# A fixed table of the order in place of a greedy plan: attention, a feed-forward layer and a soft mixture of experts on one Trainium2 core

## The chip, the core and the metric

The kernel runs on one core of one Trainium2 chip. The metric is the device time of one execution in microseconds (us), the median of several runs. A core has five engines, each with its own queue of instructions that are worked off in order: TensorE (PE in the rows; its weight loads are PEld), VectorE (DVE), ScalarE (ACT), GpSimd (POOL) and SyncE (SP), which in this kernel issues every DMA. An engine that waits for a semaphore holds up all that is queued behind the waiting instruction.

## What is computed

Three stages, one after the other; the last two have weights that are shared by all tokens.

```python
# attention: q, k, v are (4, 8, 576, 64)
q_rot, k_rot = (rotate(q), rotate(k))
scores = scale * np.matmul(q_rot, k_rot.transpose(0, 1, 3, 2))
scores = scores - np.max(scores, axis=-1, keepdims=True)
attn = np.exp(scores)
attn = attn / (np.sum(attn, axis=-1, keepdims=True) + 1e-09)
x = np.matmul(attn, v)                 # then (2304, 512)
# feed-forward: w_in (512, 2048), w_out (2048, 512)
h = x @ w_in
x = (np.maximum(h, 0.0) + alpha * np.minimum(h, 0.0)) @ w_out
# soft mixture: phi (512, 32), 8 experts, 4 slots each, w1 (8, 512, 1024), w2 (8, 1024, 512)
logits = x @ phi
d = softmax(logits, 0); slot_input = d.T @ x
slot_out[e] = np.maximum(slot_input[e] @ w1[e], 0.0) @ w2[e]
return softmax(logits, 1) @ slot_out
```

## The kernel before

**Tiling.** Attention goes over 4 batches `b` and 4 pairs `p` of heads; a pair has five row blocks `s` of 128 rows (the fifth, `s == 4`, holds the last 64 rows of both heads). For each row block and head there are: the scores on TensorE (`plain`, L419, for batch 0, in float32; `scores`, L432, for the later batches, of split values) into a PSUM tile `st`, of which there are two; the row maximum on VectorE (`top`, L437); the exponential on ScalarE (`expo`, L442); sum and reciprocal on VectorE (L449, L450); the division on GpSimd (`norm`, L474). The result then has to be transposed: in batch 0 on TensorE (`turn`, L495), for the later batches by 32x32 blocks on VectorE (`block`, L482) and through device memory, with a `save` (L519, `sc<-tb`) for each row block and a `fetch` (L528, `ET<-sc`, four DMAs) for each two. `pv` (L574) multiplies with v. Before that, q and k are rotated (`prep_qk`, L322 and L330): pair 0 of batch 0 on VectorE, all others on GpSimd.

**Weights.** `prep_w` brings `w_in` and `w_out` from raw 64-bit data into tiles (L643, L645, L647 on VectorE), scales and splits them (`bnd`, `hi`, `diag` on ScalarE, `rest` L268 and L269 on TensorE), in sixteen steps that lie within batch 0 of the attention, since the first feed-forward chunk needs both.

**Feed-forward and dispatch.** The tokens are eight blocks of 256 (two a batch) and a ninth of all the last rows. Each has sixteen chunks `f` (`mm1`, L735: twelve matmuls), whose results are activated (L743 on ScalarE, L748 on VectorE), transposed, and added up in the running softmax over tokens (`dispatch_events`).

**Tail.** When the attention's buffers are free (`att_done`), SP loads `w_out` again (`wor`, L1103, 16 transfers) and all the experts' weights (`xw`, L1158) into one pool of tiles; VectorE converts `w_out` (`late_w`), TensorE forms the slots' input (`px`, L1209), the experts (`ph` L1262, `po` L1316) and the result (`pf`, L1427), and SP stores.

**What sets the order.** The kernel first makes a list of 2900 operations. Each has an engine, an estimated cost, a due time, the operations that it depends on, and the buffers (slots of a class, such as two of `st` or three of `pm`) that it takes and uses. `Plan.order` then plays the list through: at each moment an idle engine takes, of the operations that are ready and whose slots are free, the one with the earliest due time. The order in which operations were started is the order in which their instructions are written, and so the order in each engine's queue. Semaphores are set by the data: what an instruction waits for follows from the tiles that it reads and writes. At the end:

```python
    for o in plan.order():
        o.fn()
```

## Time and profile before

| | |
|---|---|
| time before, median of 3 runs (lowest to highest) | 657.65 us (656.19 to 658.19) |
| span of the profiled execution | 663.7 us |
| TensorE busy | 609.5 us (92%) |
| VectorE busy | 462.9 us (70%) |
| ScalarE busy | 373.6 us (56%) |
| GpSimd busy | 269.9 us (41%) |
| mean DMA rate | 221 GB/s, 146.6 MB |
| first matmul | at 11.64 us |
| last matmul ends | at 657.3 us |

The profiled execution is 6.1 us longer than the median of the unprofiled runs. The page gives each engine's busy time, 40 slices of the span, and the chain of work that ended last: 71% of that chain is TensorE, 9% VectorE, 8% DMA, 5% GpSimd. A matmul that runs slowly counts as busy, so a busy TensorE is not TensorE at its peak. The trace tells each instruction's start, its length and what ended the idle time ahead of it.

### The profile page before, as it was taken

To read this page: it belongs to the slowest core of one execution; us is meant where nothing else is said; L and a number is where in the kernel's file an instruction comes from. 1 tells how busy PE (TensorE), PEld (TensorE's weight loads), DVE (VectorE), ACT (ScalarE), POOL (GpSimd) and SP (SyncE) were. 2 spreads that over 40 slices of the span, in tenths; PEclk is the share of its full clock that TensorE was granted. 3 is DMA by queue.
4 is the path that set the end of the run, shared out by engine and by line. 5 is a ranking of instruction groups with operands and counts; after the bars stand their busy time and mean duration, and the time that the engine had idled before them with its cause. 6 is when DMAs were issued, how large, how long until landed. Compare 5 with 4: busy or idle time off the path is not lost.

```text
span 663.7 us, 13899 instructions
## 1 busy us (share of the span) xinstructions
PE 609.5 (92%) x5232; PEld 429.7 (65%) x5232; DVE 462.9 (70%) x1000; ACT 373.6 (56%) x900; POOL 269.9 (41%) x262
## 2 busy tenths in 40 slices
PE   1899988999999999898899989989999999997994
PEld 1554543656878687586777867778677787773352
DVE  5859496788777867886677777867663788853442
ACT  2666775676686766766758576766554232331121
POOL 0669584467446547575574644522320000001000
PEclk9778895999999999999999999999999999997996
DMA  9954263633298887878888786667643993669998
GB/s 337 339 182 147 69 221 122 199 118 108 82 250 203 252 221 213 236 231 264 226 229 206 216 235 169 190 174 176 170 128 96 375 409 137 255 254 369 403 337 287
DMA packets 70371, 146.60 MB, mean 221 GB/s; under 512 B 5921, under 2 KB 35233, under 8 KB 70305
## 3 DMA queue, kind: packets, MB, share of 16 engines
q1 hardware_dynamic: 70304, 145.72, 70.2%
q8 instruction: 41, 0.67, 0.4%
q14 instruction: 26, 0.20, 0.1%
HBM read 108.73 MB, written 29.88 MB: 209 GB/s over the span
## 4 chain that ended last, share of the span: by engine, by line
PE 71%; DVE 9%; DMA 8%; POOL 5%; ACT 3%; issue 2%; SPq 2%; POOLq 0%; DVEq 0%; ACTq 0%
PE ph L735 25%; PE pv L574 12%; PE st L432 6%; PE st L419 5%; DMA ET<-sc 3%; PE pt L754 3%; DMA xw<-in_moe_w_dram 3%; PE lg L772 3%; PE pt L495 3%; POOL xn L322 2%; PE po L1316 2%; PE pu L891 2%; PE pc L538 2%; POOL e L474 2%; DVE mm L437 2%
## 5 line engine op out<-in xcount | busy, mean ns | idle before, releaser
L474 POOL TENSOR_SCALAR e<-e,mm 128x576 f32<-128x576 f32 x144 | 121.1, 851 | 163.6 <-DVE mm L450 100.6
L735 PEld LDWEIGHTS <-w 128*128 128x128 f16 x1728 | 163.7, 98 | 33.3 <-issue 12.4
L735 PE MATMUL ph<-xt,w 128*128 128x256 f16 x1536 | 183.8, 273 | 0.5 <-DVE g L748 0.3
L437 DVE TENSOR_REDUCE mm<-st 128x1 f32<-128x576 f32 x144 | 106.4, 744 | 32.1 <-PE st L432 15.5
L442 ACT ACTIVATE e<-st,mm 128x576 f32<-128x576 f32 x144 | 106.3, 738 | 26.9 <-DVE mm L437 22.6
L743 ACT ACTIVATE rl<-ph 128x256 f32<-128x256 f32 x144 | 55.0, 382 | 91.6 <-PE ph L735 88.1
L322 POOL TENSOR_TENSOR xn<-xn,tabs 128x576 f32<-128x576 f32 x60 | 92.1, 1551 | 34.1 <-DMA xn<-in_k_dram 16.2
L748 DVE SCALAR_TENSOR_TENSOR g<-rl,oma,ph 128x256 f32<-128x256 f32 x144 | 68.0, 472 | 40.4 <-ACT rl L743 39.1
L574 PE MATMUL pv<-ET,vt 128*64 128x256 f32 x512 | 62.3, 385 | 12.2 <-DMA ET<-sc 5.7
L432 PE MATMUL st<-ks,qs 128*128 128x288 f32 x384 | 72.5, 314 | 0.5 <-ACT e L442 0.5
L482 DVE STREAM_TRANSPOSE tb<-e 128x512 f32<-128x512 f32 x96 | 66.8, 700 | 5.6 <-POOL e L474 4.1
L419 PE MATMUL st<-ks 64*128 64x288 f32 (+1 forms) x168 | 51.0, 498 | 14.0 <-DVE ks L330 11.6
L432 PEld LDWEIGHTS st<-ks,qs 128*128 128x128 f32 x384 | 55.2, 192 | 4.5 <-issue 2.0
L574 PEld LDWEIGHTS pv<-ET,vt 128*64 128x64 f32 x512 | 35.3, 136 | 33.1 <-ACT qs L340 4.2
L419 PEld LDWEIGHTS st<-ks 64*128 64x128 f32 (+1 forms) x168 | 27.9, 210 | 28.6 <-DVE ks L330 11.6
L584 ACT ACTIVATE xt<-pv,vb 128x256 f16<-128x256 f32 x32 | 15.1, 473 | 43.8 <-PE pv L574 43.8
L759 ACT ACTIVATE gt<-pt 128x512 f32<-128x512 f32 x56 | 33.1, 596 | 11.5 <-PE pt L754 10.9
L325 POOL TENSOR_TENSOR xn<-xn 128x576 f32<-128x576 f32 x24 | 36.2, 1508 | 1.0
L449 DVE TENSOR_SCALAR mm<-mm 128x2 f32<-128x2 f32 (+1 forms) x80 | 28.5, 357 | 11.2 <-ACT e L442 10.8
L495 PE MATMUL pt<-idf,e 128*128 128x128 f32 x192 | 33.3, 307 | 3.2 <-POOL e L474 2.9
L495 PEld LDWEIGHTS pt<-idf,e 128*128 128x128 f32 x192 | 24.9, 158 | 16.3 <-POOL e L474 8.9
L587 DVE SCALAR_TENSOR_TENSOR xt<-pv,vb,xt 128x256 f16<-128x256 f32 x32 | 15.4, 481 | 28.1 <-ACT xt L584 27.9
(181 smaller groups left out, 896.6 us busy)
## 6 DMA issues: line engine op xcount, KB each, us to landing
sc<-tb SPq DMA_DIRECT2D x48, 512.0 KB, 4.6
ET<-sc SPq DMA_DIRECT2D x96, 256.0 KB, 5.7
xw<-in_moe_w_dram SPq DMA_DIRECT2D x42, 512.0 KB, 9.9
xn<-in_k_dram SPq DMA_DIRECT2D x16, 576.0 KB, 5.7
xn<-in_q_dram SPq DMA_DIRECT2D x16, 576.0 KB, 4.1
wraw<-in_moe_w_in_dram SPq DMA_DIRECT2D x8, 1024.0 KB, 9.8
wraw<-in_w_out_t_dram SPq DMA_DIRECT2D x8, 1024.0 KB, 5.2
wor<-in_moe_w_out_dram SPq DMA_DIRECT2D x16, 512.0 KB, 10.4
```

Of the source, the lines that this page charges most:

```text
L322: eng.tensor_tensor(e["x"][:, w], e["x"][:, w], tabs[:, (0 if z == "q" else 2) + w], ALU.mult)
L419: nc.tensor.matmul(st[to, j, at:at + w], x, k[rows, z:z + w], start=True, stop=True)
L432: nc.tensor.matmul(st[:, j, 0:288], r["q"][:, 768 * h + 128 * s:768 * h + 128 * s + 128].bitcast(F32R), r["k"][:, a, h, ks].bitcast(F32R), ...
L437: nc.vector.tensor_reduce(c["mm"][:, h:h + 1], c["st", h][:, :, 0:288], axis=AX.XY, op=ALU.max, negate=True)
L442: nc.scalar.activation(c["e"][:, h].rearrange("p (a n) -> p a n", a=2), c["st", h][:, :, 0:288], AF.Exp, bias=c["mm"][:, h:h + 1], accum_o ...
L474: nc.gpsimd.tensor_scalar(c["e"][:, h], c["e"][:, h], c["mm"][:, 6 + h:7 + h], 1.0, ALU.mult, ALU.mult)
L482: nc.vector.transpose(out=c["tb"][:, :, h].rearrange("p (q m) j -> p q m j", q=4), in_=c["e"][:, h, 64 * h:64 * h + 512].rearrange("p (m q ...
L495: nc.tensor.transpose(c["pt", h][:, i], c["e"][:, h, 64 * h + 128 * i:64 * h + 128 * i + 128], idf)
L574: nc.tensor.matmul(pv[r], v[k, 4 * h + i if i < 4 else 8], x, start=(i == 0), stop=(i == 4))
L735: nc.tensor.matmul(ph, wi[j][:, wp, kc, 128 * fo:128 * fo + 128], xt[:, xp, kc, :], start=(n == 0), stop=(n == 3 * KC - 1),)
L743: nc.scalar.activation(c["r"], c["ph"], AF.Relu, scale=-1.0)
L748: nc.vector.scalar_tensor_tensor(blk["g", j][:, fo, :], c["r"], oma[:, f:f + 1], c["ph"], ALU.mult, ALU.add)
```

## The change

The class `Plan` no longer plays the list through. Its `order` unpacks a table, a string of some 6,000 characters, that gives for each place the number of the operation that stands there. The 2900 operations, their tiles and their functions stay the same, and each engine gets the same instructions as before; only their order differs. The lists of dependencies get the entries that the greedy play had kept by itself (an activation after the one that allocates its tile, transposes of a group after the first, turns on the two `h1` buffers); they are used to assert that the table respects them. The first lines of the table stand for all of it.

```diff
-import bisect
-import heapq
+import base64
+import zlib
+ORDER = (
+    "c-mc72S5}@7v48}1-RqrN*BdO5yW0l6jT%g5*3x-SQ0fP(HMJ)Eo!167+Wl{`-"
...
         for d in deps:
             d.after.append(o)
-        o.wait += len(deps)
+        o.deps, o.wait = o.deps + list(deps), o.wait + len(deps)
...
     def order(self):
-        ready = {o.eng: [] for o in self.ops}
-        free = {e: 0.0 for e in ready}
...
-        while events:
...
-                    o = next((o for o in ready[e] if self.fits(o)), None)
...
+        raw = zlib.decompress(base64.b85decode(ORDER))
+        n, at, order = len(raw) // 2, 0, []
+        for lo, hi in zip(raw[:n], raw[n:]):
+            at = (at + lo + 256 * hi) % 65536
+            order.append(self.ops[at])
+        done, room, left = set(), dict(self.room), {}
...
+        for o in order:
+            assert all(d in done for d in o.deps) and o not in done, "an operation stands before one that it needs"
...
-        o = op(DVE, 480, d, act, [o, oma_op], uses=[s_pm, s_r, s_g])
+        o = op(DVE, 480, d, act, [o, oma_op, blk["g_op"][4 * j] if fo else None], uses=[s_pm, s_r, s_g])
...
-            blk["gt_op"].append(op(ACT, 600, due + 100 if late else d, turned, [o], uses=[s_pt, s_gt]))
+            blk["gt_op"].append(op(ACT, 600, due + 100 if late else d, turned, [o, blk["gt_op"][f // 8 * 4] if f % 8 > 1 else None], uses=[s_pt, s_gt]))
...
+    turns = []
+
+    def in_turn(take, *users):
+
+        for old in turns[-1:]:
+            plan.also(take, [old[0]])
+        for old in turns[-2:-1]:
+            plan.also(take, old)
+        turns.append([take, *users])
...
-            x = op(PE, 430, D2 - 10, turn, [x], takes=[s_pm], uses=[s_pm, s_h])
+            x, h = op(PE, 430, D2 - 10, turn, [x], takes=[s_pm], uses=[s_pm, s_h]), x
+            in_turn(h, x)
```

Within the operations a line of the changed kernel stands 16 lines higher than before: L403 there is L419 here, L503 is L519, L512 is L528.

**Place 1, the start of the program.** SP's queue from its first DMA, before; `tabs` are the tables of the rotation (k's first, then q's), `xn` the raw k or q of a pair, `vt` v, `wraw` raw weights:

```order
L235 DMA tabs<-in_rope_dram 128x1152
L319 DMA xn<-in_k_dram 128x1152
L235 DMA tabs<-in_rope_dram 128x1152
L319 DMA xn<-in_q_dram 128x1152
L291 DMA vt<-in_v_dram 128x576 x2
L621 DMA wraw<-in_moe_w_in_dram 128x4x512
L291 DMA vt<-in_v_dram 128x576
```

and now (the first `tabs` are q's, the second k's):

```order
L219 DMA tabs<-in_rope_dram 128x1152
L303 DMA xn<-in_k_dram 128x1152
L303 DMA xn<-in_q_dram 128x1152
L275 DMA vt<-in_v_dram 128x576
L219 DMA tabs<-in_rope_dram 128x1152
L605 DMA wraw<-in_moe_w_in_dram 128x4x512
L275 DMA vt<-in_v_dram 128x576 x3
```

The second table now comes behind q and behind one load of v. On VectorE the rotation follows, before (k, then q, each two products and a sum) and now (four products, q's first, then k's sum and q's sum):

```order
L322 TENSOR_TENSOR xn<-xn,tabs 128x576 x2
L330 TENSOR_TENSOR ks<-xn 128x576
L322 TENSOR_TENSOR xn<-xn,tabs 128x576 x2
L330 TENSOR_TENSOR ks<-xn 128x576
L437 TENSOR_REDUCE mm<-st 128x1
```

```order
L306 TENSOR_TENSOR xn<-xn,tabs 128x576 x4
L314 TENSOR_TENSOR ks<-xn 128x576 x2
L627 TENSOR_SCALAR w_164<-wraw 128x8x128
L629 SCALAR_TENSOR_TENSOR w_164<-wraw,w_164 128x8x128
L421 TENSOR_REDUCE mm<-st 128x1
```

Two steps of the first weight conversion moved ahead of the first row maximum.

**Place 2, TensorE at the start of batch 0.** `st<-ks` are scores, `pt<-idf,e` the transposes of finished rows, `rest` the remainder of a weight tile, `top` a maximum over partitions. Before:

```order
L419 MATMUL st<-ks 128x288 x8
L229 MATMUL top<-idf,vb 128x128
L229 MATMUL top<-idf,mws 128x128
L495 MATMUL pt<-idf,e 128x128 x8
L538 MATMUL pc<-idf,e 128x128
L419 MATMUL st<-ks 128x288 x4
L268 MATMUL rest<-w_177,dg 128x512
```

Now:

```order
L403 MATMUL st<-ks 128x288 x8
L213 MATMUL top<-idf,mws 128x128
L403 MATMUL st<-ks 128x288 x4
L479 MATMUL pt<-idf,e 128x128 x4
L522 MATMUL pc<-idf,e 128x128
L252 MATMUL rest<-w_164,dg 128x512
L253 LDWEIGHTS neg
L253 MATMUL rest<-w_164,neg 128x512
L479 MATMUL pt<-idf,e 128x128 x4
```

The third row block's scores moved ahead of the transposes of the first, and the first weight remainder between these transposes.

**Place 3, SP in batch 2, pair 1.** `sc<-tb` is a save, `ET<-sc` a fetch of two saved row blocks (four DMAs), the first fetch here belongs to pair 0. Before:

```order
L528 DMA ET<-sc 32x8x256 x4
L519 DMA sc<-tb 128x1024
L319 DMA xn<-in_k_dram 128x1152
L519 DMA sc<-tb 128x1024
L291 DMA vt<-in_v_dram 128x576
L363 DMA ks<-xn 64x576 x4
L519 DMA sc<-tb 128x1024
L528 DMA ET<-sc 32x8x256 x4
L519 DMA sc<-tb 128x1024
```

Now:

```order
L512 DMA ET<-sc 32x8x256 x4
L503 DMA sc<-tb 128x1024
L275 DMA vt<-in_v_dram 128x576
L503 DMA sc<-tb 128x1024
L303 DMA xn<-in_k_dram 128x1152
L512 DMA ET<-sc 32x8x256 x4
L503 DMA sc<-tb 128x1024 x2
```

The fetch of pair 1 stood behind the third row block's save and a stack of four DMAs; now it follows the second save with one load between, and the third save is behind it.

## Rows read from the trace of the kernel before

**Rows 1.** The page: busy us of each engine, share of span, instructions.

```profile
PE 609.5 (92%) x5232; PEld 429.7 (65%) x5232; DVE 462.9 (70%) x1000; ACT 373.6 (56%) x900; POOL 269.9 (41%) x262
```

**Rows 2.** Busy time by stretch: PE, PEld, DVE, ACT, POOL; then clock, DMA share, GB/s.

```profile
0.00:157.10 157.10, 133.41 (x670) 75.78 (x670) 114.69 (x210) 99.20 (x223) 93.41 (x76) 0.86 0.55 187
157.10:514.00 356.90, 341.53 (x3078) 264.87 (x3076) 259.83 (x570) 236.46 (x585) 173.86 (x181) 1.00 0.72 197
```

**Rows 3.** The same view of three stretches in batch 0.

```profile
25.06:42.12 17.06, 15.20 (x41) 7.94 (x41) 10.75 (x20) 9.97 (x20) 13.59 (x11) 0.50 0.71 248
62.60:72.85 10.25, 10.25 (x42) 6.16 (x41) 7.70 (x16) 6.05 (x14) 9.40 (x8) 0.50 0.66 224
100.15:117.22 17.07, 15.29 (x36) 6.65 (x36) 9.88 (x16) 8.88 (x20) 8.25 (x6) 0.50 0.32 109
```

**Rows 4.** Chain that ended last: start us, us, what.

```profile
31.07 2.21 PE st L419 x4
...
117.66 1.16 PE st L419 x4
...
157.31 1.34 PE ph L735 x12
```

**Rows 5.** TensorE's waits, 11 to 157 us: us in total, times, longest.

```profile
PE rest L268 <- ACT dg L262: 4.0, 3, 2.5
PE pt L495 <- POOL e L474: 2.9, 5, 1.5
PE st L419 <- ACT e L442: 2.2, 2, 1.7
```

**Rows 6.** TensorE in order of time: start, us, what, [idle before].

```profile
26.71 2.08 PE L268 MATMUL rest<-w,dg 128*128 128x512 f32 x2 [2.52 <-ACT dg L262]
...
61.61 0.66 PE L495 MATMUL pt<-idf,e 128*128 128x128 f32 x4 [1.46 <-POOL e L474]
...
100.45 2.08 PE L268 MATMUL rest<-wx,dg 128*128 128x512 f32 x2 [1.37 <-ACT dg L262]
```

**Rows 7.** Groups of TensorE by shape: busy us, mean ns, idle ahead, releasers.

```profile
L574 PE MATMUL pv<-ET,vt 128*64 128x256 f32 x512 | 62.3, 385 | 12.2 <-DMA ET<-sc 5.7 <-DVE qs L347 2.8 <-ACT qs L340 1.7
```

**Rows 8.** TensorE in order of time, batch 2, pair 1.

```profile
300.38 0.77 PE L432 MATMUL st<-ks,qs 128*128 128x288 f32 x4
...
330.72 1.95 PE L574 MATMUL pv<-ET,vt 128*64 128x256 f32 x16 [2.79 <-DVE qs L347]
```

**Rows 9.** SP in order of time, the same place.

```profile
313.60 0.32 SPq L519 DMA_DIRECT2D sc<-tb  x1
...
320.94 2.33 SPq L528 DMA_DIRECT2D ET<-sc  x4
```

**Rows 10.** VectorE in order of time, the start.

```profile
6.37 1.43 DVE L322 TENSOR_TENSOR xn<-xn,tabs 128x576 f32<-128x576 f32 x2 [3.78 <-DMA xn<-in_k_dram]
...
9.37 1.43 DVE L322 TENSOR_TENSOR xn<-xn,tabs 128x576 f32<-128x576 f32 x2 [0.79 <-DMA xn<-in_q_dram]
...
10.83 0.76 DVE L330 TENSOR_TENSOR ks<-xn 128x576 f32<-128x576 f32 x1
```

**Rows 11.** TensorE's waits over the span, the row of later batches' scores.

```profile
PE st L432 <- ACT e L442: 0.5, 2, 0.4
```

**Rows 12.** Busy time by stretch, the tail.

```profile
540.00:560.00 20.00, 20.00 (x291) 16.07 (x288) 17.34 (x42) 6.25 (x19) 0.00 (x0) 1.00 0.68 269
...
620.00:640.00 20.00, 19.61 (x254) 9.80 (x250) 6.90 (x31) 4.27 (x9) 0.00 (x0) 1.00 1.01 391
```

**Rows 13.** VectorE and GpSimd in order of time, the start of batch 0.

```profile
15.91 1.22 DVE L645 SCALAR_TENSOR_TENSOR w<-wraw,w 128x1024 int32<-128x1024 int32 x1
...
22.13 4.18 POOL L322 TENSOR_TENSOR xn<-xn,tabs 128x576 f32<-128x576 f32 x2 [1.95 <-DMA xn<-in_k_dram]
...
22.74 2.31 DVE L645 SCALAR_TENSOR_TENSOR w<-wraw,w 128x1024 int32<-128x1024 int32 x1
...
43.86 1.41 POOL L322 TENSOR_TENSOR xn<-xn,tabs 128x576 f32<-128x576 f32 x1
```

More of the change, by code (lines that the diff above doesn't have):

```diff
@@ L73, in also @@
             d.after.append(o)
-        o.wait += len(deps)
-    @staticmethod
-    def lag(a, b):
-        if a.eng is None or b.eng is None:
-            return 0
-        if a.eng == b.eng == "DMA" and b.back:
-            return 3300
-        if a.eng == b.eng:
-            return {"DVE": 127, "POOL": 102}.get(a.eng, 0)
-        if b.eng == "DMA":
-            return 1420
-        if b.eng == "PE":
-            return {"DMA": 2400, "POOL": 240}.get(a.eng, 230)
-        return {"DMA": 2400, "PE": 230 if b.eng == "ACT" else 197, "POOL": 65}.get(a.eng, 160)
@@ L90, in pe_end @@
-    def pe_end(self, at, cost):
-        while cost > 1e-6:
-            edge = self.window + 3413.0
-            if at >= edge:
-                if self.busy >= 0.96 * 3413.0:
-                    self.warm = True
-                elif self.busy < 0.33 * 3413.0:
-                    self.warm = False
-                self.window, self.busy = edge, 0.0
-                continue
-            k = 1.0 if self.warm else 2.0
-            step = min(cost * k, edge - at)
-            at, cost, self.busy = at + step, cost - step / k, self.busy + step
-        return at
@@ L155, in fits @@
-    def fits(self, o):
-        need = {}
-        for s in o.takes:
-            need[s.cls] = need.get(s.cls, 0) + 1
-        return all(self.room[c] >= k for c, k in need.items())
+        o.deps, o.wait = o.deps + list(deps), o.wait + len(deps)
+    def order(self):
+        raw = zlib.decompress(base64.b85decode(ORDER))
[4 more added lines that the diff above has]
+        done, room, left = set(), dict(self.room), {}
+        for o in self.ops:
+            for s in set(o.uses):
+                left[s] = left.get(s, 0) + 1
+        for o in order:
+            assert all(d in done for d in o.deps) and o not in done, "an operation stands before one that it needs"
+            for s in o.takes:
+                room[s.cls] -= 1
+                assert room[s.cls] >= 0, "a buffer is taken before it is free"
+            for s in set(o.uses):
+                left[s] -= 1
+                room[s.cls] += not left[s]
+            done.add(o)
+        assert len(order) == len(self.ops)
+        return order
```

89 lines of the change are left out of this document (46 added, 43 removed).

## The prediction

> **What bounds the kernel now.** I read the page's busy times first: TensorE 92% of the span, no other engine over 70% [rows 1]. The table by stretch then says where the missing time lies. Up to 157.1 us, where the first feed-forward chunk starts, TensorE works 133.4 us at a mean clock of 0.86; from there to 514 us it works 341.5 of 356.9 us at full clock [rows 2]. So the first stretch is the loose one, and there two things are lost. One is the clock: in three stretches of 17.06, 10.25 and 17.07 us the granted clock is 0.50, the 1.2 GHz level, while TensorE is busy for 15.20, 10.25 and 15.29 us, 40.7 us together [rows 3]. The same scores take 2.21 us there and 1.16 us at 2.4 GHz [rows 4]; if all work there shrank so, 40.7 x (1 - 1.16 / 2.21) = 19.3 us is the whole price of the slow clock. The other is waiting: 4.0 us for the diagonal that the weight remainder needs, 2.9 us for rows that GpSimd divides, 2.2 us for the exponential [rows 5], about 11.5 us with the view's small rows. The clock fell at 25.06, 62.60 and 100.15 us [rows 3]; each time TensorE had just been idle or was so, for 2.52, 1.46 and 1.37 us [rows 6].
>
> In the long middle stretch nearly all waiting is one kind: 12.2 us ahead of `pv`, which needs the fetched rows [rows 7]. What the row names there as releaser (a VectorE line) had been done; it was the transfer: one such `pv` starts at 330.72 us after 2.79 us of idleness [rows 8], 9.8 us after its fetch began to be issued at 320.94 us [rows 9].
>
> The same instructions run before and after, so only waits and the clock can change. I count the order's pieces between two operations and price each at the median that it has in the trace at full clock, as 1.16 us for a score of batch 0 and 1.34 us for a feed-forward chunk [rows 4]. Such a sum is the cover that an operation has while its input is made elsewhere.
>
> **The start: +1.4 us.** Before, the first score waits for q's last sum, which ends at 10.83 + 0.76 = 11.59 us. Two tables and two inputs of equal size are loaded; the first two are there at 6.37 us and all four at 9.37 us [rows 10], so one takes 1.5 us. Now the table that k needs is fifth, behind a load of v of half that size: all is there at 9.37 + 0.75 = 10.12 us. Behind it stand two products and two sums, 1.43 + 2 x 0.76 = 2.95 us [rows 10], so the first score can start at 13.07 us instead of 11.6. I take +1.4 us (bounds 0 and +3, if the weight steps that VectorE now does ahead of the first maximum wait for their load).
>
> **Waits in batch 0: -6 us.** For the 36 transposes of batch 0 the cover between a row's score and its transpose is 10.6 us in the mean before and 14.5 us now, and it is larger in 34 of 36. The one that waited until 61.61 us [rows 6] had 14.4 us of cover and has 15.9 us now, 1.5 us more, which is its wait. So the TensorE side is done well. But VectorE works 114.7 us and GpSimd 93.4 us of these 157.1 us [rows 2], and if TensorE runs ahead, they become late. I take half of the 11.5 us (bounds -11.5 and 0).
>
> **The clock in batch 0: -8 us.** If the waits ahead of the three falls go, the falls may go with them; nothing says all will, and the middle stretch has longer waits, as the 2.79 us [rows 8], with the clock at 1.00 throughout [rows 2]. I take somewhat under half of 19.3 us (bounds -19.3, and +5 for another fall of 10 us at half clock). VectorE stays a floor: 114.7 us of work in a stretch that would then be 157.1 + 1.4 - 6 - 8 = 144.5 us is 79%, against 73% now, which is feasible.
>
> **The fetches: -10 us.** Two things changed for the 24 `pv` that wait for a fetch. First, SP: before, the fetch stood in 14 of 24 places behind a save of the next row block or a load whose release comes more than 1 us of TensorE work later than its own, now in 4; the third place of the order shows one. In the trace its save was issued at 313.60 us and the fetch 7.3 us later [rows 9]. Second, the cover from the last score to `pv` is 23.3 us in the mean before and 28.0 us now. For the `pv` at 330.72 us it is 25.1 and 30.3 us: its scores ended at 301.15 us, so it needed 29.6 us [rows 8]. Five of the 24 have less cover than before, the two of batch 2, pair 3 by 3.1 and 0.7 us, so I leave 2 of the 12.2 us [rows 7] (bounds -12.2 and -4).
>
> **Score buffers: +2 us.** With two `st` tiles a score waits until the exponential two scores earlier is done. In the middle stretch the cover for that is shorter than the time which the softmax took in the trace at 19 places, by 29 us in sum; before it was 6 places and 7 us, which cost 0.5 us [rows 11], since VectorE and ScalarE then serve that row earlier. 29 x 0.5 / 7 = 2 us (bounds 0 and +29).
>
> **The tail: +2 us.** The last attention `pv` now has 458 us of TensorE work ahead of it and its like, where it had 451, so the tail's loads start 7 us of work later. Between 540 and 560 us the DMA engines are busy for 0.68 of the time, so part of the delay is taken up by idle transfers; from 620 to 640 us they are full at 1.01 [rows 12], and there a delay shows. SP also has loads of the second expert matrix among those of the first. By the count both orders have issued the same number of loads when the last dispatch starts. I take +2 us (bounds -3 and +7).
>
> **Sum:** 1.4 - 6 - 8 - 10 + 2 + 2 = -18.6 us, on the profiled execution 663.7 - 18.6 = 645.1 us. That execution is 6.1 us longer than the median of 657.65 us, and I take the same step off the median: 639.0 us.
>
> **Rivals.** *VectorE and GpSimd take the first stretch back.* VectorE's shift of the raw weights takes 1.22 us alone and 2.31 us while GpSimd multiplies, whose two products take 4.18 us there, and one 1.41 us elsewhere [rows 13]. Packed closer, both overlap more; if the 14 us of waits and clock are eaten so, 1.4 - 10 + 2 + 2 = -4.6 us and 653.0 us. The Trainium skill (SBUF — State Buffer, section Who interferes with whom) has a rule that makes this likelier: the port pair that VectorE shares with GpSimd is locked for a whole instruction by whichever begins first. By that rule the loss grows with every overlap that a closer order makes; the rows above agree that such pairs exist, and no run here yet shows how many more there will be. For this rival speaks that VectorE is already the second most used engine; against it, that its share only has to rise from 73% to 79%. Chance 0.2.
>
> *The first stretch is cured.* All 11.5 us of waits and all 19.3 us of slow clock go, and all 12.2 us ahead of `pv`: 1.4 - 11.5 - 19.3 - 12.2 + 2 + 2 = -37.6 us, 620 us. VectorE would then be busy for 114.7 of 127.7 us, 90%; that hardly leaves room for its own waits. Chance 0.08.
>
> *The score buffers bind.* The place is the middle stretch: if VectorE and ScalarE don't serve the closer scores sooner, the 29 us are paid in full instead of 2: -18.6 + 27 = +8.4 us and 666 us. It turns the sign when more than 20.6 of the 29 us are paid. Against it is the row of 0.5 us. Chance 0.08 for slower by it, and 0.04 more for slower by late loads in the tail, which would need over 20 us there.
>
> *The order changes, the time doesn't.* Gains in the middle are given back where SP or the tail's full DMA engines set the pace anyway: 657.65 us. Chance 0.05.
>
> **Chances and range.** The forecast, between about 628 and 649 us, has 0.55. Faster by over 0.3% (about 2 us, what a measurement of this kernel can tell from no change): 0.55 + 0.2 + 0.08 and a little of what lies between, 0.83; within 0.3%: 0.05; slower: 0.12. For 8 in 10 the range holds the forecast, the first rival and the nearer part of the second: 625 to 655 us.
>
> **What would show it.** In the changed profile the first matmul should start near 13.0 us; the first feed-forward chunk (L735 moved up 16 lines, so L719) near 144 us instead of 157.1; one or two stretches at clock 0.50 within batch 0 instead of three; TensorE's idle time ahead of `pv` (L558) near 2 us instead of 12.2; its wait for the exponential in the later batches near 2 us. The distance from the last `pv` to the end, 150 us before, should stay within some 5 us. The prediction is wrong if the first chunk doesn't start earlier although the waits are gone (then VectorE or GpSimd sets the pace), if the clock falls as often as before, or if what batch 0 gains is lost while TensorE waits for the experts' weights.

## The result, and the profile after

The changed kernel takes 625.87 us (median of 4 runs, 620.67 to 630.32) beside 657.12 us for the kernel before: a ratio of 0.947 (95% interval 0.941 to 0.954). Two more measurements gave 0.948 (0.945 to 0.952) and 0.945 (0.942 to 0.949). The forecast of 639.0 us had the direction right; of the 31 to 37 us by which the three medians fell it had 18.6. On the 657.65 us that it started from, the three ratios give 621.6 to 623.7 us, below the 625 us at which its range ended. The kernel before is the less steady of the two: in four later calls its median was 661 to 662 us, with single runs from 654.62 to 668.47 us, and its profiled execution, with a span of 663.7 us, lies in that spread (a span in a trace is some 2 us shorter than the time of the same execution). Some runs below are compared across these four calls; the kernel before had 661.0 to 661.8 us in each of them. The changed kernel stays between 620.67 and 630.32 us.

The page's busy times after (as [rows 1]):

```profile
PE 582.6 (94%) x5232; PEld 421.9 (68%) x5232; DVE 458.4 (74%) x1000; ACT 370.8 (60%) x900; POOL 264.8 (43%) x262
```

TensorE has the same 5232 instructions and is busy for 26.9 us less: for the most part a slow clock had counted as work. The table by stretch (columns as in [rows 2]; the cuts are the first feed-forward chunk and the end of the last attention `pv`), of the first trace of the changed kernel:

```profile
0.00:135.00 135.00, 114.51 (x670) 67.47 (x671) 111.21 (x199) 96.64 (x219) 88.27 (x73) 0.99 0.60 209
135.00:481.50 346.50, 344.50 (x3140) 271.23 (x3140) 262.83 (x586) 238.74 (x593) 173.79 (x184) 1.00 0.75 206
481.50:618.90 137.40, 123.63 (x1424) 83.16 (x1424) 84.38 (x215) 35.39 (x89) 2.75 (x5) 0.97 0.90 341
```

and of a later one (the run `after_third` below):

```profile
0.00:137.40 137.40, 112.06 (x670) 65.88 (x671) 111.66 (x199) 96.91 (x219) 91.95 (x73) 1.00 0.60 206
137.40:485.00 347.60, 344.53 (x3140) 271.32 (x3138) 264.00 (x586) 239.03 (x593) 174.40 (x184) 1.00 0.76 206
485.00:622.80 137.80, 123.09 (x1428) 83.21 (x1424) 84.47 (x215) 35.46 (x89) 2.75 (x5) 0.98 0.90 340
```

Against [rows 2]: in the first stretch the same 670 matmuls are busy for 114.5 and 112.1 us instead of 133.4 us, at a clock of 0.99 and 1.00 instead of 0.86. In the middle TensorE idles 2.0 and 3.1 us instead of 15.4 us, although 62 more matmuls now lie in it: five feed-forward chunks of 1.34 us [rows 4] and two matmuls of 0.22 us, an estimated 7.1 us of work. The tail lasts 137.4 and 137.8 us where it was 149.7 us; 7.1 us of that is the work that moved.

The clock column of these tables leaves something out. A trace has no record of the clock before its first rise, and the column counts that time as 1.00. The first rise stands at 21.64 us in the first trace of before, and at 30.33, 27.22 and 27.95 us in the traces of `after`, `after_again` and `after_third`. Until then TensorE works at half speed, the 1.2 GHz level: in the first trace of before one score follows the other after 0.48 us ahead of the rise and after 0.24 us behind it, and in the first trace of the changed kernel the same two matmuls take, ahead of the rise and later:

```profile
26.16 1.92 PE L252 MATMUL rest<-w,dg 128*128 128x512 f32 x2
...
82.57 1.12 PE L252 MATMUL rest<-w,dg 128*128 128x512 f32 x2
```

With this start and the falls together, TensorE is busy at half speed for 8.3 + 40.7 = 49.0 us of batch 0 before, for 15.6 + 3.4 = 19.0 us in the first trace of the changed kernel (which has one fall, of 3.41 us at 64.47 us) and for 12.8 us in the later one. If half of each is the price of the slow clock, it fell from 24.5 us to 9.5 and 6.4 us. The new order ends the falls, but its slow start is longer.

VectorE at the start (as [rows 10]): the second pair of products waits for the table that comes fifth, and the first score starts 12.72 us after the beginning instead of 11.64 us.

```profile
7.60 1.43 DVE L306 TENSOR_TENSOR xn<-xn,tabs 128x576 f32<-128x576 f32 x2 [6.70 <-DMA xn<-in_q_dram]
9.77 1.43 DVE L306 TENSOR_TENSOR xn<-xn,tabs 128x576 f32<-128x576 f32 x2 [0.75 <-DMA tabs<-in_rope_dram]
11.23 1.43 DVE L314 TENSOR_TENSOR ks<-xn 128x576 f32<-128x576 f32 x2
```

TensorE's groups by shape (as [rows 7]), `pv` and the later batches' scores, with their idle time behind the second bar:

```profile
L416 PE MATMUL st<-ks,qs 128*128 128x288 f32 x384 | 73.2, 316 | 0.0
L558 PE MATMUL pv<-ET,vt 128*64 128x256 f32 x512 | 62.7, 385 | 0.8 <-ACT xn L322 0.6 <-ACT ET L488 0.2
```

The 12.2 us ahead of `pv` are 0.8, and the scores, which the forecast charged 2 us more for their two buffers, wait for nothing.

The terms of the forecast's sum beside what the two traces show against the first trace of before (all in us; waits in batch 0 are the first stretch less busy time less the start; the clock in batch 0 is the estimate just given, and what is left of the busy time's fall stands in a row of its own; the middle and the tail are reckoned with the moved 7.1 us put back):

| term | forecast (bounds) | first trace | later trace |
|---|---|---|---|
| start | +1.4 (0 to +3) | +1.1 | +1.7 |
| waits in batch 0 | -6 (-11.5 to 0) | -4.3 | 0.0 |
| clock in batch 0 | -8 (-19.3 to +5) | -15.0 | -18.1 |
| other busy time in batch 0 | none | -3.9 | -3.3 |
| middle: fetches -10, score buffers +2 | -8 | -17.5 | -16.4 |
| tail | +2 (-3 to +7) | -5.2 | -4.8 |
| sum | -18.6 | -44.8 | -40.9 |

The sums are larger than the 31 to 37 us of the medians, since the first trace of before is of a long execution. Against its second trace (`before_again`, span 660.7 us) the later trace is 37.9 us shorter; there the middle idled 12.8 us instead of 15.4 us, and the tail lasted 147.0 us.

### The profile page after: what moved, and what is told of

It is laid out like the page before. It is cut to its first block, busy times and chain, and to the rows that moved or that the text cites. A ratio compares the mean times of both kernels' runs of the same rounds, so it can differ in the third digit from the quotient of the medians.

```text
span 618.9 us, 13875 instructions
## 1 busy us (share of the span) xinstructions
PE 582.6 (94%) x5232; PEld 421.9 (68%) x5232; DVE 458.4 (74%) x1000; ACT 370.8 (60%) x900; POOL 264.8 (43%) x262
## 4 chain that ended last, share of the span: by engine, by line
PE 83%; ACT 6%; DVE 4%; DMA 3%; issue 2%; SPq 1%; POOL 0%; DVEq 0%; ACTq 0%; POOLq 0%
PE ph L719 29%; PE pv L558 13%; PE st L416 8%; PE st L403 5%; PE pt L738 4%; PE lg L756 3%; PE pt L479 3%; PE ph L1256 2%; PE po L1311 2%; PE rest L252 2%; PE pu L875 2%; PE pc L522 2%; DMA vt<-in_v_dram 2%; ACT e L426 1%; PE st L412 1%
## 5 line engine op out<-in xcount | busy, mean ns | idle before, releaser
L719 PEld LDWEIGHTS <-w 128*128 128x128 f16 x1728 | 165.1, 98 | 29.0 <-issue 6.9
L458 POOL TENSOR_SCALAR e<-e,mm 128x576 f32<-128x576 f32 x144 | 114.7, 807 | 159.6 <-DVE mm L434 75.7
L719 PE MATMUL ph<-xt,w 128*128 128x256 f16 x1536 | 181.4, 273 | 1.0 <-issue 0.8
L306 POOL TENSOR_TENSOR xn<-xn,tabs 128x576 f32<-128x576 f32 x60 | 94.7, 1591 | 24.8 <-DMA xn<-in_k_dram 17.6
L466 DVE STREAM_TRANSPOSE tb<-e 128x512 f32<-128x512 f32 x96 | 65.2, 695 | 5.2 <-POOL e L458 5.0
L403 PE MATMUL st<-ks 64*128 64x288 f32 (+1 forms) x168 | 41.0, 468 | 16.7 <-DVE ks L314 12.7
L403 PEld LDWEIGHTS st<-ks 64*128 64x128 f32 (+1 forms) x168 | 23.8, 197 | 29.8 <-DVE ks L314 12.7
L743 ACT ACTIVATE gt<-pt 128x512 f32<-128x512 f32 x56 | 32.9, 596 | 15.4 <-PE pt L738 14.8
L738 PE MATMUL pt<-idf,g 128*128 128x128 f32 x224 | 34.2, 277 | 0.3 <-DVE g L732 0.3
L334 ACT ACTIVATE ks<-xn 64x576 fp32r<-64x576 f32 x48 | 32.6, 680 | 0.8
L433 DVE TENSOR_SCALAR mm<-mm 128x2 f32<-128x2 f32 (+1 forms) x80 | 22.1, 277 | 13.0 <-ACT e L426 12.6
L479 PE MATMUL pt<-idf,e 128*128 128x128 f32 x192 | 30.5, 288 | 1.1 <-POOL e L458 0.4
```

The costliest lines, as they stand in the source:

```text
L306: eng.tensor_tensor(e["x"][:, w], e["x"][:, w], tabs[:, (0 if z == "q" else 2) + w], ALU.mult)
L403: nc.tensor.matmul(st[to, j, at:at + w], x, k[rows, z:z + w], start=True, stop=True)
L458: nc.gpsimd.tensor_scalar(c["e"][:, h], c["e"][:, h], c["mm"][:, 6 + h:7 + h], 1.0, ALU.mult, ALU.mult)
L466: nc.vector.transpose(out=c["tb"][:, :, h].rearrange("p (q m) j -> p q m j", q=4), in_=c["e"][:, h, 64 * h:64 * h + 512].rearrange("p (m q ...
L719: nc.tensor.matmul(ph, wi[j][:, wp, kc, 128 * fo:128 * fo + 128], xt[:, xp, kc, :], start=(n == 0), stop=(n == 3 * KC - 1),)
L738: nc.tensor.transpose(c["pt"][:, t, i, :], blk["g", j][:, fo - 1 + i, 128 * t:128 * t + 128], idf)
```

## The experiments

The table of the order is a list of operation numbers, so an experiment on it needs no other code. Where a part of the old order stands in the new code, three of the stated dependencies that the old order doesn't keep in the tail are left out (the turns on the two `h1` buffers, and that of a transpose behind the one before); the waits themselves follow from the tiles in any case. L numbers are those of the changed kernel.

### Both kernels again

The two kernels unchanged (no edit).

> The changed kernel once more, with its trace. Theory A (the order itself keeps the clock up): the granted clock stays at 0.50 for under 10 us of batch 0 again, the first feed-forward chunk starts within 5 us of 135.0 us, and the median is 622 to 627 us. Theory B (the falls of the clock come by chance, whatever the order): in some execution a fall of 10 us or more stands in batch 0 again, the mean clock comes under 0.98 and the first chunk starts 5 to 15 us later.

Measured: 625.31 us (623.19 to 627.31). First chunk at 136.3 us, no fall of the clock before 600 us.

> The changed kernel again, for the comparison with the two above on the same chip: 623 to 628 us. Theory wait for the clock: no stretch at 0.50 of over 7 us before 600 us.

Measured: 624.78 us (623.61 to 627.77), again no fall before 600 us.

> The kernel before once more, for a second trace and the granted clock of several executions. Theory wait for the clock: falls in batch 0 again within 3 us of the waits near 24, 60 and 99 us, 25 to 50 us at 0.50 in all, of varying length, and with it the time varies by 5 us or more at a mean clock of 0.95 to 0.97. Theory chance: falls at other places, or none.

Measured: 659.29 us (654.62 to 664.91). The busy time by stretch in its trace:

```profile
0.00:157.60 157.60, 133.16 (x670) 75.50 (x670) 115.32 (x210) 99.14 (x223) 94.39 (x76) 0.86 0.55 187
25.63:35.87 10.24, 8.73 (x17) 4.09 (x18) 7.33 (x14) 7.31 (x14) 9.31 (x8) 0.50 0.66 228
59.76:70.00 10.24, 10.24 (x41) 5.93 (x41) 7.01 (x16) 5.62 (x12) 9.39 (x8) 0.50 0.68 224
97.31:121.20 23.89, 21.73 (x56) 9.98 (x57) 13.30 (x21) 12.05 (x27) 8.92 (x7) 0.50 0.38 128
```

The three falls stand within 3 us of the places of [rows 3], with 44.4 us at half clock in all beside 44.4 us there, in other shares: the place is the order's, the length varies. A fourth, of 3.41 us, begins at 305.52 us in the middle, behind a wait of 2.31 us for a fetch. So the falls of the old order's start are no chance, and neither is it that the new one has few: of the six traces with the new order up to the first chunk (three of the changed kernel, and those of `start_new`, `tail_old` and `fetch_back` below) three have none in batch 0, and three have one each, of 3.41, 6.83 and 3.41 us.

### The three stretches by themselves

```diff
-the old order
+start_new: the new order up to the first chunk (616 operations), then the others in the old order
+start_old: the old order up to the first chunk (624 operations), then the others in the new order
+tail_old: the new order up to the last attention pv, then the others in the old order
```

> The new order up to the first feed-forward chunk, the old order behind it. In the profiles the first chunk moved from 157.15 to 135.02 us, 22.1 us. Theory A (that stretch's gain is made by its own order): first chunk near 135 us, and a median 13 to 22 us under that of the kernel before, 635 to 644 us (13, since the profiled execution of before was about 9 us longer than its median, which I put on its clock). Theory B (chance): the first chunk anywhere from 135 to 157 us and the median within 5 us of before.

Measured: 652.07 us (646.50 to 660.12), a ratio of 0.986 (0.982 to 0.989). Its first chunk starts at 136.4 us, at a clock of 1.00; behind the seam it meets a wait that neither kernel has, and a fall (busy time by stretch, and TensorE in order of time):

```profile
0.00:136.40 136.40, 111.99 (x670) 66.06 (x671) 111.15 (x199) 96.75 (x219) 91.87 (x73) 1.00 0.60 207
143.18:153.42 10.24, 5.53 (x29) 3.59 (x29) 5.96 (x13) 5.82 (x11) 7.47 (x6) 0.50 0.59 164
```

```profile
147.89 1.94 PE L479 MATMUL pt<-idf,e 128*128 128x128 f32 x8 [8.30 <-DVE g L732]
```

So the stretch's gain is made by its own order, as theory A had it, and the median is 8 us above A's range since the seam costs 8.3 us of waiting and some 3 us of slow clock. Its old tail lasts 147.5 us from the last `pv`, 2.2 us less than in the first trace of before, whose clock fell there.

> The old order up to the first feed-forward chunk, the new order behind it. Theory A (the stretches add up): clock at 0.50 for 30 us or more of batch 0, first chunk near 155 us, and TensorE's idle time ahead of pv under 2 us as in the changed kernel; the middle and the tail give 17 and 5 us, so the median is 633 to 640 us. Rival (the middle only runs without waits because the new first stretch leaves its loads further ahead): pv waits over 5 us again and the median is over 645 us.

Measured: 643.47 us (640.22 to 646.50). The first stretch is the old one (four falls of 10.24 us, clock 0.87), the middle nearly the new one: TensorE waits 1.9 us for fetches.

```profile
0.00:156.90 156.90, 133.06 (x670) 75.66 (x671) 116.03 (x210) 99.38 (x222) 93.34 (x76) 0.87 0.55 187
```

The median is 3.5 us above theory A's range. It is 18.2 us slower than the changed kernel of the same call: the first stretch's worth, and the middle and tail give the other 18.3 of 36.5 us. The rival (the middle needs the new start) falls.

> The new order up to the last attention pv, the old order behind it. In the profiles the distance from the last pv to the end fell from 149.7 to 137.4 us, of which 9.2 us is TensorE work that now lies ahead of it and 3.1 us is a slow clock from 601.9 to 608.7 us that did not come again. If the order of the loads in the tail matters, this kernel is 3 to 8 us slower than the changed one; if it does not (my forecast gave the new tail a loss of 2 us), it is within 2 us of it or up to 2 us faster.

Measured: 631.14 us (628.05 to 631.70), 5.8 us slower than the changed kernel. Its tail lasts 143.6 us, with 4.8 us of idleness ahead of the last chunk, 2.5 us of it for one activation right behind the seam. The old tail in `start_new`, without a seam there, less 7.1 us of work lasts 140.4 us, against 137.4 to 138.0 us in three traces of the changed kernel. So the new tail is worth an estimated 2 to 3 us, and the rest of the 5.8 us is put down to the seam. The trace has a fall of 6.83 us at 85.97 us, in a part of the order that is the changed kernel's.

### What brings the clock down

```diff
 L213 MATMUL top<-idf,mws 128x128
+L479 MATMUL pt<-idf,e 128x128 x4
 L403 MATMUL st<-ks 128x288 x2
 L479 MATMUL pt<-idf,e 128x128 x4
 L403 MATMUL st<-ks 128x288 x2
-L479 MATMUL pt<-idf,e 128x128 x4
```

`pause`: this and two more steps like it, in the new order.

> The new order with three steps of batch 0 moved earlier on TensorE (near 45, 54 and 93 us), so that each waits for its input by an estimated 2.5 to 3.1 us, 8.4 us together; the same instructions otherwise. Theory wait (a wait of over a microsecond in batch 0 brings the half clock): the granted clock falls to 0.50 within 4 us of at least two of them, some 5 us of lost time each beside the waits, so 634 to 645 us against 625.3 us. Rival (the falls of the old order come from something else, its mix of work or chance): at most one fall, and only the waits are paid, 626 to 634 us.

Measured: 632.30 us (631.98 to 632.51), 7.0 us above 625.3 us: within the rival's range of time, but with the falls that theory wait had named. Two of the three steps waited, and both brought a fall (TensorE in order of time, then busy time by stretch):

```profile
48.31 0.65 PE L479 MATMUL pt<-idf,e 128*128 128x128 f32 x4 [2.81 <-POOL e L458]
...
98.14 1.22 PE L252 MATMUL rest<-wx,dg 128*128 128x512 f32 x1 [2.24 <-ACT dg L246]
```

```profile
50.21:57.04 6.83, 6.82 (x17) 3.49 (x16) 6.73 (x9) 3.02 (x6) 6.75 (x6) 0.50 0.27 86
97.99:108.23 10.24, 10.09 (x42) 4.63 (x43) 5.72 (x8) 3.24 (x9) 1.24 (x1) 0.50 0.42 121
```

The third step, near 54 us, did not wait, and there is no fall there. The first chunk starts at 145.5 us, 8.1 us later than in `after_third`: that is the whole loss. TensorE's idle time in the first stretch is the same within 0.1 us, since the added waits of 5.0 us took the place of others, as of the one of 3.1 us near 84 us. So the loss is all busy time, and half of the 16.9 us of work in the two falls is 8.5 us. All four runs show it: their mean clock is 0.976 to 0.979, where the six of `after_again` have 0.986 to 0.994.

```diff
             c["p"] = ps_m.tile([128, 128], F32, tag="pm", name="top")
+            for _ in range(more):
+                nc.tensor.transpose(c["p"], idf, idf)
             nc.tensor.matmul(c["p"], src.to_broadcast([128, 128]), idf, start=True, stop=True)
```

`fill`: the same added at six steps in the order of `start_old`.

> The old order in batch 0 and the new one behind it (643.5 us, four falls of 10.24 us there), with 25 transposes of the identity added on TensorE in front of six operations that wait (near 24, 57, 95, 96, 100 and 102 us, 7.4 us of waiting together), so that it works there; they write where the waiting operation then writes its own result. Theory wait: the falls at 26, 60 and 98 us do not come, and the time falls by 3 x 5 us or more, to 622 to 631 us, though work was added. Rival (the falls come from something else): three or four falls as before, 641 to 650 us.

Measured: 638.11 us (637.10 to 639.39), 5.4 us under `start_old` with 25 instructions more. The added transposes took only 0.14 us each (eight of them 1.10 us), so about half of the waiting was filled. The falls are three of 3.41, 6.83 and 3.41 us instead of four of 10.24 us:

```profile
0.00:148.70 148.70, 123.84 (x695) 72.57 (x695) 118.59 (x210) 98.50 (x222) 94.42 (x76) 0.95 0.58 198
30.82:34.23 3.41, 3.41 (x8) 1.25 (x7) 3.08 (x8) 2.03 (x4) 3.41 (x4) 0.50 0.76 259
99.08:105.91 6.83, 6.39 (x20) 2.37 (x17) 1.20 (x3) 2.88 (x7) 0.99 (x1) 0.50 0.48 154
136.63:140.04 3.41, 3.41 (x20) 2.60 (x21) 3.35 (x5) 1.70 (x6) 3.29 (x3) 0.50 0.00 0
```

The wait near 57 us, cut from 1.46 to 0.76 us, brought none; the three falls follow waits that were left, of 1.38, 1.37 and 0.99 us. Neither range was met, but the direction is that of the wait theory: with work in the place of waiting the clock fell for 13.7 us instead of 41.0 us. The mean clock of the four runs is 0.985 to 0.990, that of the six of `start_old` 0.960 to 0.970.

Over all 17 traces there are 42 falls before 540 us; 41 began in a wait of TensorE of over 0.9 us or within 4 us behind it, one behind a wait of 0.42 us. In batch 0 (from 20 to 145 us) waits of 0.85 to 2 us were so followed in 27 of 44 cases, later in the program in none of 83. All 27 belong to the old order's start; the one such wait that the new start has, of 1.2 to 1.3 us near 33 us, was followed by a fall in none of eight traces, and its wait of 3.1 us near 84 us in two of five. A fall nearly always comes with a wait, then, but what stands around it decides too, and that stays open.

### The fetches

```diff
 L275 DMA vt<-in_v_dram 128x576
+L512 DMA ET<-sc 32x8x256 x4
 L347 DMA ks<-xn 64x576 x4
-L503 DMA sc<-tb 128x1024
-L512 DMA ET<-sc 32x8x256 x4
-L503 DMA sc<-tb 128x1024
+L503 DMA sc<-tb 128x1024 x2
```

`fetch_ahead`: SP's queue of the old order at this and seven more places (here the third place of the order).

> The old order everywhere, with eight of the 24 fetches moved ahead on SP of the save or loads that they stood behind; nothing else moves. In the old trace TensorE waits ahead of pv for 12.2 us, about 8.1 us of it at five of these eight places (at 231, 302, 328, 384 and 444 us) and the rest at places left as they were. Theory SP (the place in SP's queue makes the wait): idle ahead of pv falls to under 5 us, and the time by 5 to 8 us against the kernel before. Theory cover (the distance on TensorE from the scores to pv makes it): idle ahead of pv stays over 9 us and the time within 3 us.

Measured: 655.28 us (653.63 to 667.89), a ratio of 0.990 (0.984 to 0.996). In its trace, of the execution of 667.89 us, the idle time ahead of `pv` is 7.0 us, 0.6 us of it at the eight places, where it was 8.1 us; this lies between the two theories' numbers. But TensorE's idle time in the whole middle stayed at 14.9 us. Hence a second look, and the other half of the term by itself:

> The eight fetches ahead on SP once more, for a second trace. In the first one idle ahead of pv fell to 7.0 us with none at the eight places, but TensorE's whole idle time in the middle stretch stayed at 14.9 us against 15.4, since it waited 3.3 us for VectorE's activation ahead of a chunk and 1.6 us for a division. If that is a rule, the idle time of the middle is again within 2 us of 15 us; if it was that run's chance, it is under 11 us and the time 5 us under the kernel before.

Measured: 663.45 us (659.20 to 669.08) beside 661.04 us, a ratio of 1.004 (1.000 to 1.009): no gain. The middle's stretch, `pv`, and TensorE's waits there:

```profile
154.35:511.50 357.15, 342.21 (x3077) 265.07 (x3076) 261.85 (x570) 236.79 (x585) 174.17 (x181) 1.00 0.72 197
```

```profile
L558 PE MATMUL pv<-ET,vt 128*64 128x256 f32 x512 | 63.6, 391 | 7.8 <-DMA ET<-sc 5.1 <-DVE mm L433 1.4 <-ACT rl L727 0.8
```

```profile
PE pv L558 <- DMA ET<-sc: 5.1, 5, 2.1
PE ph L719 <- DVE g L732: 2.9, 3, 2.0
PE pc L522 <- POOL e L458: 1.6, 1, 1.6
```

14.9 us of idleness again. Waits of up to 2.0 us for an activation and one of 1.6 us for a division, which the old trace doesn't have, and longer ones at fetches that were left in place, make up for what the eight places gave.

```diff
 L275 DMA vt<-in_v_dram 128x576
-L512 DMA ET<-sc 32x8x256 x4
 L347 DMA ks<-xn 64x576 x4
 L503 DMA sc<-tb 128x1024
+L512 DMA ET<-sc 32x8x256 x4
+L503 DMA sc<-tb 128x1024
```

`fetch_back`: the new order with 17 fetches one save later.

> The new order with 17 of the 24 fetches moved behind the next save on SP (two of them past a load besides). Theory SP: TensorE idles ahead of pv for 5 us or more, against 0.8 us in the changed kernel, and the time is 630 us or more, against 625.3 us. Theory cover: the 28.0 us between scores and pv take up the delay, idle ahead of pv stays under 2.5 us and the time is within 2 us of 625.3 us.

Measured: 668.46 us (666.28 to 670.66), 43 us over the changed kernel. Idle time by shape, one of the seven waits, SP there and the clock:

```profile
L558 PE MATMUL pv<-ET,vt 128*64 128x256 f32 x512 | 70.6, 422 | 32.5 <-DMA ET<-sc 31.8 <-ACT ec L526 0.6
```

```profile
333.65 2.83 PE L558 MATMUL pv<-ET,vt 128*64 128x256 f32 x12 [7.97 <-DMA ET<-sc]
```

```profile
312.16 12.74 SPq L503 DMA_DIRECT2D sc<-tb  x2
325.07 2.23 SPq L512 DMA_DIRECT2D ET<-sc  x4
```

```profile
330.06:336.89 6.83, 3.23 (x16) 1.90 (x16) 0.00 (x0) 0.00 (x0) 0.00 (x0) 0.50 0.90 223
```

The two saves took SP until 324.9 us, and the fetch behind them landed only with the `pv` at 333.65 us. The cover, 28.0 us in the mean, took up ten of the 17 delays; at the other seven TensorE waited. Four of those waits, of 5.4 us or more, brought the clock down in the middle too, where [rows 2] had shown it at 1.00 throughout. SP's order is necessary for the new middle.

```diff
+L416 MATMUL st<-ks,qs 128x288 x4
+L738 MATMUL pt<-idf,g 128x128 x4
 L558 MATMUL pv<-ET,vt 64x256 x8
 L558 MATMUL pv<-ec,vt 64x256 x2
```

`cover`: the old order, each of the 24 `pv` behind the pieces that followed it (at this place a chunk of L719 more), with its readers right behind it. `cover_ahead` is this on top of `fetch_ahead`.

> The old order everywhere, with the 24 pv that wait for a fetch moved later on TensorE by two to four pieces, so that 4.8 us more of work in the mean lies between the scores and pv (the new order has 4.6 us more); what reads pv's result moves with it, SP's order stays but for six neighbours. Theory SP: idle ahead of pv stays over 6 us (12.2 us in the first old trace, 9.6 in the second). Theory cover: under 3 us. If no other wait comes in its place, the stretch from the first feed-forward chunk to the last attention pv shrinks by as much as pv waits less.

Measured: 704.97 us (695.66 to 708.62), a ratio of 1.058 (1.048 to 1.067). The wait ahead of `pv` is gone, and the middle lasts 398.9 us:

```profile
L558 PE MATMUL pv<-ET,vt 128*64 128x256 f32 x512 | 62.3, 385 | 0.0
```

```profile
157.00:555.90 398.90, 355.76 (x3108) 266.66 (x3107) 251.93 (x572) 233.60 (x585) 172.23 (x181) 1.00 0.65 176
```

```profile
PE st L416 <- ACT e L426: 7.0, 7, 1.7
PE pc L522 <- POOL e L458: 4.0, 6, 1.2
```

ScalarE shows how such a wait comes about; in order of time:

```profile
304.17 0.47 ACT L568 ACTIVATE xt<-pv,vb 128x256 f16<-128x256 f32 x1 [3.48 <-PE pv L558]
304.54 0.59 ACT L743 ACTIVATE gt<-pt 128x512 f32<-128x512 f32 x1
305.02 0.75 ACT L426 ACTIVATE e<-st,mm 128x576 f32<-128x576 f32 x1
```

ScalarE stands 3.48 us before the step that reads the later `pv`, with an activation and the next row's exponential queued behind it. Nearly all of TensorE's idle time of 43.1 us is in 56 waits, 20 of them of over 1 us, for scores, chunks and transposes. These waits are in part the edit's own: the readers moved with `pv` on ScalarE and VectorE, and no run has them at other places.

> Both at once: the eight fetches ahead on SP and the 24 pv 4.8 us later, all else in the old order. Theory sum: idle ahead of pv under 1.5 us and the middle stretch 9 to 12 us shorter than the old one's 356.9 us (with the work that moves in or out of it counted off). Rival (other waits take the place of those for the fetch, as for VectorE's activations): the middle stretch within 4 us of the old one's.

Measured: 713.39 us (710.23 to 719.16), a ratio of 1.080 (1.072 to 1.087); `pv` waits 0.0 us, the middle lasts 408.1 us and idles 50.1 us, so both theories fail. Both parts of the term take waits ahead of `pv` away, and as edited here neither alone nor both together shorten anything. Up to the last attention `pv` the new order changes what stands ahead of some 520 operations on TensorE, 590 on ScalarE and 720 on VectorE; with all of these the wait went and no other came in its place. Which of them are needed stays open.

### Repairing what is left

In five of the six traces with the new order up to there (`after_again`, `after_third`, `start_new`, `tail_old`, `fetch_back`) TensorE waits 3.1 us near 84 us; in the first trace it doesn't. GpSimd and VectorE in order of time, in that trace:

```profile
81.78 1.30 POOL L457 TENSOR_SCALAR e<-e,mm 128x64 f32<-128x64 f32 x1
```

```profile
80.57 2.32 DVE L629 SCALAR_TENSOR_TENSOR wx<-wraw,wx 128x1024 int32<-128x1024 int32 x1
```

and in `after_third`, with TensorE:

```profile
83.86 2.41 POOL L457 TENSOR_SCALAR e<-e,mm 128x64 f32<-128x64 f32 x1
```

```profile
83.81 2.35 DVE L631 SCALAR_TENSOR_TENSOR wx<-wraw,wx 128x1024 int32<-128x1024 int32 x2
```

```profile
87.61 0.66 PE L479 MATMUL pt<-idf,e 128*128 128x128 f32 x4 [3.08 <-POOL e L458]
```

In `after_third` the division begins 0.05 us behind the first of two weight shifts on VectorE (1.21 us each) and ends 0.11 us behind the second; in the first trace it began halfway through one such instruction, ended 0.19 us behind it, and TensorE's transposes had their input in time. The Trainium skill (SBUF — State Buffer, section Who interferes with whom) says that whichever of the two engines begins first holds the shared ports for its whole instruction; that one shape takes 1.30 and 2.41 us, each time to the end of what VectorE had begun (one instruction, and two that follow each other at once), agrees.

The five traces are alike in this: in each of them VectorE begins 0.04 to 0.05 us ahead of the division, so it is no tie that falls now one way, now the other. In the first trace VectorE stood elsewhere in its queue: the row maximum that begins at 78.37 us in `after_third` began at 82.82 us there, 4.4 us later, behind a wait of 1.03 us for ScalarE near 75 us and three weight steps that took 6.49 us instead of 3.54 us. The clock had fallen at 64.47 us in that trace; that this fall made VectorE late is not shown.

```diff
 L306 TENSOR_TENSOR xn<-xn,tabs 128x576 x2
+L457 TENSOR_SCALAR e<-e,mm 128x64
+L458 TENSOR_SCALAR e<-e,mm 128x576
 L309 TENSOR_TENSOR xn<-xn 128x576
-L457 TENSOR_SCALAR e<-e,mm 128x64
-L458 TENSOR_SCALAR e<-e,mm 128x576 x3
+L458 TENSOR_SCALAR e<-e,mm 128x576 x2
```

> The new order with one step moved on GpSimd: the division of the fifth row block of pair 1 in batch 0 stands ahead of a sum of the rotation instead of behind it (near 81 us); its input has been ready since 72.6 us. In four of the five traces with the new start TensorE waits 3.08 us there, while the division of 128x64 takes 2.41 us beside VectorE's weight shift (1.30 us in the first trace, without the wait). Theory pair (GpSimd waits for VectorE's weight shift, and the wait is a matter of which begins first): the wait is gone, and the time is about 3 us under the changed kernel in the same call. Rival (the wait only moves to the next transposes, since VectorE and GpSimd have the same work to do): within 1 us of it.

Measured: 626.15 us (625.63 to 627.00), against 624.78 us for the changed kernel in the same call. The wait is still there, with another cause, and brought a fall of 6.83 us:

```profile
88.35 1.09 PE L479 MATMUL pt<-idf,e 128*128 128x128 f32 x4 [3.83 <-ACT w L257]
```

The division ran earlier; the sum of the rotation that it passed now ran later, ScalarE waited for that sum, and the step of L257 that the row names stood behind it on ScalarE. This is the rival's mechanism; the time, 1.4 us above the changed kernel, lies just outside its range of 1 us.

```diff
+L219 DMA tabs<-in_rope_dram 128x1152
 L275 DMA vt<-in_v_dram 128x576
-L219 DMA tabs<-in_rope_dram 128x1152
```

`better`: this on SP, the step of `norm_first`, and two steps on TensorE near 28 and 32 us.

> The same step on GpSimd and three more moves in the new order: k's table is loaded ahead of the first v (the first score some 0.7 us earlier), one set of transposes stands ahead of a score that waits 1.32 us for an exponential near 32 us (0.6 us), and one score ahead of a weight remainder that waits 0.60 us near 28 us. If each of these is on the path that sets the end, 3.1 + 0.7 + 0.6 + 0.6 = 5 us under the changed kernel in the same call; if VectorE takes them back, within 1 us of norm_first.

Measured: 625.58 us (625.33 to 626.96). The first score starts at 11.97 us, 0.75 us earlier than in the first trace of the changed kernel, and the second row block's scores wait for the same exponential until 16.87 us (the changed kernel: 16.85 us):

```profile
16.87 1.80 PE L403 MATMUL st<-ks 64*128 64x288 f32 x4 [2.61 <-ACT e L426]
```

The two waits near 28 and 32 us went too, and the first chunk starts at 138.0 us all the same, behind a wait of 3.82 us and a fall of 6.83 us near 86 us as in `norm_first`. No version here beats the changed kernel.

## Why the prediction was wrong

The two places were right, and so was the direction of their terms; most sizes were not, and one mechanism is shown only in part. By the steps:

**The start** was forecast at +1.4 us and measured +1.1 and +1.7 us, by the wait that was named. `better`, with k's table loaded earlier again, is no faster, which the forecast hadn't weighed.

**The waits in batch 0** were half right for the wrong reason. The cover of the transposes did grow, and the waits near 24, 60 and 97 us went; but in most traces the collision of VectorE and GpSimd puts 3.1 us back near 84 us, so that the sum is 12.0 us as before. This is the first rival's mechanism, at one place instead of over the whole stretch. It didn't take the gain back: VectorE was busy for 111.7 of 137.4 us, 81%.

**The clock in batch 0** is the first term that failed: -8 us, measured -15.0 and -18.1 us by the estimate above. The step argued that the falls "may go", and that longer waits in the middle left the clock at 1.00, and took under half. The old order has its three falls at the same places within 6 us in all seven traces with that start, and `pause` and `fill` show that falls come with waits there and shrink with them. The edit took away the three waits that the falls followed, and nearly all of the falls' price went. The middle's counterexample doesn't hold for batch 0, where waits of a length that did nothing in the middle brought falls in 27 of 44 cases; and the clock fell in the middle of `before_again` too. But that so few falls would come in their place couldn't be known from the waits, since the new order's own wait of 3.1 us brought one in two of five traces. The forecast's whole price, 19.3 us, left out the first 8.3 us of work, which ran at half speed too and which the new order made more; and it had no term for the 3.3 to 3.9 us that TensorE is busy less besides. For a part of these the matmuls lie closer: eight scores in a row take 1.70 us at 82.25 us in `after_third`, where four by themselves take 1.16 us [rows 4].

**The fetches** were the second: -10 us forecast, and +2 us for the score buffers. The waits ahead of `pv` went as forecast; the scores wait for nothing (0.0 us), so the count of shortfalls was no cost. The stretch gained 16.4 to 17.5 us: 12.3 to 13.4 us of idleness, and the rest in pieces that are busy for 3.0 us more where 7.1 us of work came in, which no step had counted. And the step's two causes do not explain the gain by themselves: SP's order is needed (`fetch_back`), but each of the two, put into the old order, nearly emptied the wait at its places and gained nothing, or lost 44 us. What the forecast lacked is that a wait removed alone lets the next one in; that the whole order didn't do so here couldn't be read from those two counts. What in it keeps the other waits away stays open.

**The tail** was forecast at +2 us and measured -4.8 to -5.2 us. Of this an estimated 2.2 us is a fall of the clock at 601.9 us in the first trace of before, and the other 2 to 3 us the tail itself; the later start of its loads cost nothing that shows.

**Rivals.** The score buffers binding and the late loads did not come. What came is nearest to the rival called the first stretch is cured, for its clock and its `pv`, with 8% too little of a chance: it was discounted since VectorE would have had to be busy for 90% of the stretch, but it was reckoned with all waits gone too, and these stayed. The step from the profiled execution to the median (6.1 us, and some 8 us if the span's 2 us are counted in) did little harm: the old kernel's own spread is wider than that.

## What to carry to other kernels

A slow clock that follows named waits should be priced with those waits: here an edit took away the wait ahead of each fall, and nearly the whole cost of the falls went, though a stretch where longer waits mostly left the clock alone had seemed to speak against it. How fast the work runs is best read from the same instruction at two places, since a column of the clock can lack its start. Before one wait is repaired by hand, list what stands behind the moved operation and its readers on every queue, since the gain goes to whichever of them is next late; an order that changed on all engines at once was worth some 17 us in the middle, where the single repairs tried here were worth nothing. And an order is to be judged over several traces, since the first one lacked a wait of 3.1 us that five others have.

## What the runs showed of the hardware

TensorE ran at half speed from its first matmul at 11.64 us until 21.64 us in the first trace of before, and until 27.22 to 30.33 us in three traces of the changed kernel. One fetch placed behind one save more cost up to 8.0 us on TensorE and brought a fall of the clock, where 28.0 us of cover stood against it in the mean. In `fetch_back` the granted clock fell in the middle of the program as well (0.50 for 6.83 to 10.24 us) behind waits of 5.4 to 8.0 us; the Trainium skill (TensorE: Matmul & The Clock Gate, section HAM oscillation — how this bites in real kernels) tells of waits for DMA between short stretches of matmuls that bring the lower clock back, and these waits were for DMA. In batch 0 waits for other engines did the same, and in the middle of `cover` and `cover_ahead` waits of 2.61, 3.25 and 3.71 us for VectorE and GpSimd (0.50 for 3.41 to 6.83 us).
